# Cosine attention and feed-forward on one core: key tiles added up in float32 before the softmax totals

## The chip, the cores and the metric

The kernel runs on one core of a Trainium2 chip. The core's engines are TensorE (PE, with its weight loads as PEld), VectorE (DVE), ScalarE (ACT), GpSimd (POOL) and SyncE (SP), which issues most DMAs. The metric is the device time of one execution in microseconds. Before the change it is 416.8 us (median of three runs, 416.55 to 417.8).

## The reference

Queries, keys and values have 8 batches, 12 heads, 448 positions and 64 columns. Queries and keys are normalised, and the scores pass a softmax; the result goes through two matrices with a leaky ReLU between them.

```python
q_n = q / (np.linalg.norm(q, axis=-1, keepdims=True) + 1e-06)
k_n = k / (np.linalg.norm(k, axis=-1, keepdims=True) + 1e-06)
scores = np.matmul(q_n, k_n.transpose(0, 1, 3, 2)) / tau
scores = scores - np.max(scores, axis=-1, keepdims=True)
attn = np.exp(scores)
attn = attn / (np.sum(attn, axis=-1, keepdims=True) + 1e-09)
x = np.matmul(attn, v)                 # then (8 * 448, 768): heads side by side
h = x @ w_in                           # 768 x 2048
out = np.maximum(0.01 * h, h) @ w_out  # 2048 x 768
```

## The kernel before, in words

The order of the instructions on every engine is the order in which the Python program writes them; the framework adds the waits on semaphores. Two kinds of work are mixed by hand: attention, which needs TensorE, ScalarE, VectorE and GpSimd, and the feed-forward product, which is mostly TensorE.

The first two batches (twelve pairs of heads) go through an older path (`scores`, `totals`, `products`, `scale`). From the third batch on, the kernel works in *units* of two head pairs, 18 in all, in *groups* of one or two units, ten in all (`GROUPS`, `UNITS`). A unit has seven *key tiles*: `quad_tiles` makes the scores of 64 keys of each of its four heads by eight products of 64x32 (line 417, eight tiles of the array) into two PSUM banks, and ScalarE takes their exponential (line 423) into a bf16 tile `pe` of 128x896, kept in `pq[u, i]`.

`group_products(g, e)` (line 442) multiplies the seven tiles of a group. With `e = None` the weights are ones: the result is the sum over the keys, the softmax's denominator, from 56 products (seven tiles, four strips, two halves of the rows). With `e` 0 or 1 the weights are the even or odd columns of v. `group_logs` (line 451) and `group_inverse` (line 454) turn the sums into their inverses on ScalarE, and `group_scale` (lines 467 and 473) multiplies products and inverses on VectorE into `xT`, the feed-forward input.

The main loop runs over 42 *visits* of three key tiles. In a visit VectorE first normalises a preparation slot (`normalise`, lines 253 to 260: a slot is the queries or the keys of a unit), transposes it (line 306), and sums the squares of the next slot (line 232); SP moves the transposed tile to its place and loads a later slot. GpSimd first copies one element of the normalised tile (`hold`, line 616), which makes it wait for VectorE's multiply of line 260, and then squares the slot after next (line 216). TensorE makes one tile's scores, a *part* of a finished group if one is due, the other two tiles' scores, and then a share of feed-forward work. `parts` puts the totals (`e = None`) and the products `e = 0, 1` of a group into the visits after its last tile; `at[c]` says from which visit the chunk `c` of the feed-forward work may run, and `level` and `share` spread that work over the visits.

The feed-forward work is in eight chunks of 384 or 512 rows: `first` (line 494, six products into one bank, then the leaky ReLU on ScalarE, line 505) and `second` (line 531, sixteen products into one bank, then a copy to `osb` on VectorE, line 541, and a DMA on SP). PSUM has eight banks, dealt out by `banks`, oldest first.

After the loop come the last group's totals and products with the rest of the work, and the last chunk.

The lines that say what a sentence can't:

```python
for e in (None, 0, 1)[: 1 + len(js)]:
    last += 1
    parts[last] = (g, e)
```

Of the kernel before, what the change touches and what calls it, by code (L numbers as in the profile page):

```python
# [8 lines left out]
F32 = mybir.dt.float32  # L9
BF16 = mybir.dt.bfloat16  # L10
AF = mybir.ActivationFunctionType
ALU = mybir.AluOpType
# [4 lines left out]
def kernel(  # L17
# [10 lines left out]
    nc = tc.nc  # L28
    B, H, S, D = q.shape
# [9 lines left out]
    NQ = NPAIR // 2  # L39
# [3 lines left out]
    WARM = 20  # L43
    NEWQ = 2 * NQ
    PER = 3
    assert REM == 64 and D == 64

    ctx.enter_context(tc.manual_schedule())
    cpool = ctx.enter_context(tc.tile_pool(name="consts", bufs=1))
    ldp = ctx.enter_context(tc.tile_pool(name="ld", bufs=4))  # L50
    vbp = ctx.enter_context(tc.tile_pool(name="vb", bufs=3))
    smp = ctx.enter_context(tc.tile_pool(name="small", bufs=3))
    qnp = ctx.enter_context(tc.tile_pool(name="qn", bufs=3))
    ttp = ctx.enter_context(tc.tile_pool(name="tt", bufs=2))
    qtp = ctx.enter_context(tc.tile_pool(name="qt", bufs=6))
    pep = ctx.enter_context(tc.tile_pool(name="pe", bufs=25))
    vqp = ctx.enter_context(tc.tile_pool(name="vq", bufs=2))
    rbp = ctx.enter_context(tc.tile_pool(name="rb", bufs=2))
    xtp = ctx.enter_context(tc.tile_pool(name="xt", bufs=2))
    htp = ctx.enter_context(tc.tile_pool(name="ht", bufs=1))  # L60
    osp = ctx.enter_context(tc.tile_pool(name="os", bufs=3))
# [4 lines left out]
    gp = nc.gpsimd  # L66
# [8 lines left out]
    def banks(count, keep=None):  # L75
        lo, hi = (0, 8) if not deals["apart"] else (0, 4) if count == 2 else (4, 8)
        x = min(
            (i for i in range(lo, hi, count) if not set(range(i, i + count)) & set(kept.values())),
            key=lambda i: max(age[i : i + count]),
        )  # L80
        deals["n"] += 1
        age[x : x + count] = [deals["n"]] * count
        if keep:
            kept[keep] = x
        return ps[:, x] if count == 1 else ps[:, x : x + count]
# [31 lines left out]
    OLD = 2 * NEWQ  # L117
# [51 lines left out]
    vb, vrb = {}, []  # L169

    def load_v(j):
        if j >= B * NQ:
            return
        b, jj = divmod(j, NQ)
        vb[j] = vbp.tile([128, 4, 3, D], BF16, name="v_b")
        gp.dma_start(out=vb[j], in_=main(v, b, 4 * jj, 4))

    def load_v_rem(b, heads=range(4)):
# [9 lines left out]
    UNITS = [  # L188
        (g, (2 * js[0] + x, 2 * js[-1] + x if len(js) == 2 else 2 * js[0] + 1))
        for g, js in enumerate(GROUPS) for x in range(len(js))  # L190
    ]
# [17 lines left out]
    def squares(s, eng=gp, parts=(0, 1)):  # L209
        if s >= NSLOT:  # L210
            return
        sq = sqt[s % 3]
        if s >= OLD:
            sqs[s] = sq
            x = raw[s].rearrange("p (t d) -> p t d", d=D)
            gp.tensor_tensor(sq[:, :, :D], x, x, op=ALU.mult)  # L216
            return
        sqs[s] = halves(sq.rearrange("p t d -> p (t d)"), D + 1)
        for i in parts:
            x, y = raw[s][i], sqs[s][i]  # L220
            if eng is nc.scalar:
                nc.scalar.activation(y[..., :D], x, func=AF.Square)
            else:
                eng.tensor_tensor(y[..., :D], x, x, op=ALU.mult)  # L224
# [17 lines left out]
    def roots(s):  # L242
        if s >= NSLOT:
            return
        nc.scalar.activation(ss[s], ss[s], func=AF.Ln)  # L245
        nc.scalar.activation(norms[s % 3][:, :, 0], ss[s], func=AF.Exp, scale=0.5)  # L246
# [80 lines left out]
    pe, pr = {}, {}  # L327
# [45 lines left out]
    def totals(j):  # L373
        sm = banks(1)
        strip_products(j, sm, lambda g, ki: ones, lambda g: ones_rem[:, g // 2])
        rb = rbp.tile([128, 2, S], F32, name="rb")[:, 0]
        nc.scalar.activation(rb, sm[:, :S], func=AF.Ln)
        nc.scalar.activation(rb, rb, func=AF.Exp, scale=-1.0)
        rbs[j] = rb
# [21 lines left out]
        if (j, e) in kept:  # L401
            given_back((j, e))

    pq = {}

    def quad_tiles(which):

        tiles = []
        for u, i in which:
            sc = banks(2)  # L410
            tiles.append(sc)
            for strip in range(4):
                x = qkT[UNITS[u][1][strip // 2]]
                c0 = S + 64 * i + 32 * (strip % 2)
                for a in range(2):
                    rows = slice(64 * a, 64 * a + 64)
                    nc.tensor.matmul(  # L417
                        out=sc[32 * strip : 32 * strip + 32, a, :S], lhsT=x[rows, c0 : c0 + 32],
                        rhs=x[rows, 0:S], start=True, stop=True,
                    )  # L420
        for (u, i), sc in zip(which, tiles):
            pq[u, i] = pe_tile()
            nc.scalar.activation(out=pq[u, i], in_=sc[:, :, :S], func=AF.Exp, scale=inv_tau)  # L423

    grb = {}

    def group_products(g, e):


        us = [u for u, (gg, _) in enumerate(UNITS) if gg == g]  # L430
        two = len(us) == 2
        po = banks(2)
        for i in range(7):
            for strip in range(4):
                for w in range(2):
                    x, a = strip // 2, strip % 2
                    rows = slice(64 * w, 64 * w + 64)
                    weights = ones[rows] if e is None else (
                        vq[g][rows, strip if two else a, i]
                        .rearrange("p (d e) -> p e d", e=2)[:, e if two else w ^ x]  # L440
                    )
                    nc.tensor.matmul(  # L442
                        out=po[32 * strip : 32 * strip + 32, w, :S],
                        lhsT=weights, rhs=pq[us[x if two else 0], i][rows, a, :],
                        start=(i == 0), stop=(i == 6),
                    )
        return po

    def group_logs(g, po):
        grb[g] = rbp.tile([128, 2, S], F32, name="rb")  # L450
        nc.scalar.activation(grb[g], po[:, :, :S], func=AF.Ln)

    def group_inverse(g):
# [122 lines left out]
    sqt = []  # L576
# [11 lines left out]
    nc.vector.memset(warm, 1.0)  # L588
    ones = cpool.tile([128, 32], BF16, name="ones")
    nc.vector.memset(ones, 1.0)  # L590
    ones_rem = cpool.tile([128, 2, 32], BF16, name="ones_rem")
    nc.vector.memset(ones_rem, 0.0)
    for i in range(2):
        nc.vector.memset(ones_rem[64 * i : 64 * i + 64, i], 1.0)
    for i in range(2):
        vrb.append(cpool.tile([128, NQ, 4, D], BF16, name=f"v_rem{i}"))
        nc.vector.memset(vrb[i], 0.0)
    id128 = cpool.tile([128, 128], BF16, name="id128")
    make_identity(nc, id128)
# [264 lines left out]
    visit_of = {ui: n for n, tiles in enumerate(visits) for ui in tiles}  # L864
    parts, ready, last = {}, {}, 0
    for g, js in enumerate(GROUPS):
        last = max(last, max(visit_of[u, 6] for u, (gg, _) in enumerate(UNITS) if gg == g))
        for e in (None, 0, 1)[: 1 + len(js)]:
            last += 1
            parts[last] = (g, e)  # L870
        ready.update({j: last + 1 for j in js})
# [15 lines left out]
        for n in range(len(visits))  # L887
    ]

    held = []  # L890
    fed = 0
    for n, tiles in enumerate(visits):
        s = preps.get(n, NSLOT)
        g, e = parts.get(n, (None, None))
        scaling = e is not None

        def prepare():
            if s < NSLOT:
                transposes(s)
                load_qk(s + 4)  # L900
                hold(qn[s][:, 6, 0, 0:1])
                squares(s + 2)
                sums(s + 1)

        normalise(s)
        if not scaling:
            prepare()
        quad_tiles(tiles[:1])
        if g is not None:
            po = group_products(g, e)  # L910
            if e is None:
                group_logs(g, po)
            else:
                group_scale(g, e, po)
        if scaling:
            prepare()
        quad_tiles(tiles[1:])
        if g is not None and e is None:
            group_inverse(g)
        for u, i in tiles:  # L920
            if i == 6 and u and UNITS[u][0] != UNITS[u - 1][0]:
                load_vq(UNITS[u][0])
        for c in marked:
            if at[c] == n:
                held += marked[c]
        level = min(
            (sum(loads[c] for c in loads if at[c] <= x) - fed + sum(side[n : x + 1])) / (x - n + 1)
            for x in range(n, len(visits))
        )
        share = (level - side[n]) / (4 if n == len(visits) - 1 else 1)  # L930
        now, done = [], 0
        while held:
            w = weight(held[0][0], held[0][1][0])
            if now and done + w / 2 > share:
                break
            now.append(held.pop(0)[1][1])
            done += w
        fed += done
        for fn in now[:-1]:
            fn()  # L940
        roots(s + 1)
        for fn in now[-1:]:
            fn()
    g = len(GROUPS) - 1
    group_logs(g, group_products(g, None))
    group_inverse(g)
    rest = [fn for _, (_, fn) in held]
    cut = len(rest) // 3
    for fn in rest[:cut]:
        fn()  # L950
    for e in range(2):
        group_scale(g, e, group_products(g, e))
# [39 lines left out]
```

## Time and profile before

| | before |
|---|---|
| time, median of three runs | 416.8 us |
| the profiled execution's own time | 416.43 us |
| its span | 414.6 us |
| TensorE busy | 407.1 us, 98% of the span |
| ScalarE busy | 250.2 us, 60% |
| VectorE busy | 221.5 us, 53% |
| GpSimd busy | 114.6 us, 28% |
| the totals' products (ones, line 442) | 560 products, 15.1 us busy |
| squares of 128x896 on GpSimd (line 216) | 36, mean 1695 ns |
| multiplies of 128x896 on VectorE (line 260) | 36, mean 1176 ns |

The span is the time from the first to the last instruction that the profiler shows; the execution's time is the time of the whole run. Products on different tiles of TensorE's array can run at the same time, so the sum of busy time and the time between two starts differ. The visits run from 80.9 to 344.2 us; the last multiply of line 260 starts at 302.3 us.

### The profile page before, as it was taken

To read this page: it belongs to the slowest core of one execution; us is meant where nothing else is said; L and a number is where in the kernel's file an instruction comes from. 1 tells how busy PE (TensorE), PEld (TensorE's weight loads), DVE (VectorE), ACT (ScalarE), POOL (GpSimd) and SP (SyncE) were. 2 spreads that over 40 slices of the span, in tenths; PEclk is the share of its full clock that TensorE was granted. 3 is DMA by queue.
4 is the path that set the end of the run, shared out by engine and by line. 5 is a ranking of instruction groups with operands and counts; after the bars stand their busy time and mean duration, and the time that the engine had idled before them with its cause. 6 is when DMAs were issued, how large, how long until landed. Compare 5 with 4: busy or idle time off the path is not lost.

```text
span 414.6 us, 11342 instructions
## 1 busy us (share of the span) xinstructions
PE 407.1 (98%) x4799; PEld 212.3 (51%) x4799; DVE 221.5 (53%) x387; ACT 250.2 (60%) x431; POOL 114.6 (28%) x149
## 2 busy tenths in 40 slices
PE   8899999999999999999999999999999999999997
PEld 3335555544555555544455555554445555654565
DVE  6977976855778556766474964464621301210022
ACT  5997876378657785668865688547764464004300
POOL 4875543433234132413331433122210000000000
PEclk9999999999999999999999999999999999999999
DMA  7999998775377851884275681742442100020022
GB/s 195 242 214 220 210 234 187 181 223 129 60 206 182 204 132 22 204 229 99 53 186 157 151 229 43 175 126 84 91 90 68 51 39 3 38 77 0 2 76 76
DMA packets 41964, 53.82 MB, mean 130 GB/s; under 512 B 12474, under 2 KB 32314, under 8 KB 41914
## 3 DMA queue, kind: packets, MB, share of 16 engines
q1 hardware_dynamic: 25738, 41.01, 35.0%
q0 software_dynamic: 15488, 11.80, 19.7%
q8 instruction: 37, 0.61, 0.6%
q10 hardware_dynamic: 688, 0.30, 0.2%
q14 instruction: 13, 0.11, 0.1%
HBM read 45.61 MB, written 11.01 MB: 137 GB/s over the span
## 4 chain that ended last, share of the span: by engine, by line
PE 87%; DMA 4%; ACT 3%; DVE 3%; POOL 2%; SPq 1%; issue 1%; POOLq 0%
PE ps L531 34%; PE ps L494 34%; PE ps L442 9%; PE ps L417 7%; ACT pe L355 2%; DMA qk_h<-in_k_dram 2%; PE ps L366 2%; DVE qn L270 1%; DMA xT<-in_k_dram 1%; DMA xT<-in_q_dram 1%; POOL sq L224 1%; PE ps L346 1%; POOL sq L216 1%; DVE ss L238 0%; SPq L131 0%
## 5 line engine op out<-in xcount | busy, mean ns | idle before, releaser
L531 PE MATMUL ps<-w_out_sb,hT 128*128 128x384 bf16 (+1 forms) x912 | 151.3, 324 | 0.3 <-DVE xT L397 0.3
L494 PE MATMUL ps<-xT,w_in_sb 128*128 128x384 bf16 (+1 forms) x768 | 151.1, 353 | 0.0
L423 ACT ACTIVATE pe<-ps 128x896 bf16<-128x896 f32 x126 | 108.9, 915 | 46.1 <-PE ps L417 46.1
L531 PEld LDWEIGHTS <-hT 128*128 128x128 bf16 x912 | 86.5, 98 | 64.3 <-issue 10.0
L494 PEld LDWEIGHTS <-w_in_sb 128*128 128x128 bf16 x768 | 72.6, 98 | 74.3 <-issue 9.7
L505 ACT ACTIVATE hT<-ps 128x384 bf16<-128x384 f32 (+1 forms) x128 | 67.4, 552 | 56.0 <-PE ps L494 55.0
L541 DVE COPY osb<-ps 128x384 f32<-128x384 f32 (+1 forms) x57 | 31.2, 548 | 100.7 <-PE ps L531 100.6
L216 POOL TENSOR_TENSOR sq<-qk_h 128x896 f32<-128x896 f32 x36 | 61.0, 1695 | 9.2 <-DMA qk_h<-in_k_dram 7.7
L616 POOL CAST seen<-qn 128x1 f32<-128x1 bf16 x46 | 8.5, 185 | 169.4 <-DVE qn L260 160.5
L260 DVE TENSOR_TENSOR qn<-qk_h,r 128x896 bf16<-128x896 f32 x36 | 42.4, 1176 | 1.2
L232 DVE TENSOR_REDUCE ss<-sq 128x14 f32<-128x910 f32 x36 | 38.0, 1054 | 1.1 <-POOL sq L216 1.1
L355 ACT ACTIVATE pe<-ps 128x896 bf16<-128x896 f32 x42 | 35.9, 917 | 1.8 <-PE ps L346 1.7
L417 PE MATMUL ps<-qkT 64*32 64x448 bf16 x1008 | 36.5, 353 | 0.0
L253 DVE TENSOR_REDUCE r<-norms 128x14 f32<-128x28 f32 x48 | 8.6, 178 | 48.3 <-ACT norms L246 47.7
L467 DVE TENSOR_TENSOR xT<-ps,rb 128x448 bf16<-128x448 f32 x32 | 18.4, 617 | 23.2 <-PE ps L442 21.5
L306 DVE STREAM_TRANSPOSE tt<-qn 128x448 f32<-128x448 f32 x36 | 29.6, 821 | 0.9
L442 PE MATMUL ps<-pe,vq 64*32 64x448 bf16 x1008 | 27.0, 349 | 0.0
L245 ACT ACTIVATE ss<-ss 128x14 f32<-128x14 f32 x48 | 10.3, 214 | 25.4 <-DVE ss L232 24.4
L417 PEld LDWEIGHTS <-qkT 64*32 64x32 bf16 x1008 | 13.1, 91 | 19.2 <-issue 14.5
L442 PEld LDWEIGHTS <-vq 64*32 64x32 bf16 x1008 | 14.5, 92 | 8.0 <-issue 0.3
L442 PE MATMUL ps<-pe,ones 64*32 64x448 bf16 x560 | 15.1, 349 | 0.0
L346 PE MATMUL ps<-qkT 64*64 64x448 bf16 (+1 forms) x132 | 12.9, 359 | 2.1 <-ACT pe L355 1.2
(53 smaller groups left out, 218.9 us busy)
## 6 DMA issues: line engine op xcount, KB each, us to landing
qk_h<-in_q_dram SPq DMA_DIRECT2D x36, 224.0 KB, 4.0
qk_h<-in_k_dram SPq DMA_DIRECT2D x36, 224.0 KB, 4.3
out_dram<-osb SPq DMA_DIRECT2D x20, 384.0 KB, 2.3
qkT<-tt SPq DMA_DIRECT2D x72, 56.0 KB, 3.3
qkT<-tt SPq DMA_DIRECT2D x36, 112.0 KB, 3.5
vq<-in_v_dram POOLq DMA_DIRECT2D x16, 224.0 KB, 5.0
w_in_sb<-in_moe_w_in_dram POOLq DMA_DIRECT2D x4, 768.0 KB, 11.2
w_out_sb<-in_moe_w_out_dram POOLq DMA_DIRECT2D x2, 1536.0 KB, 22.3
```

Source lines behind the costliest of these rows:

```text
L216: gp.tensor_tensor(sq[:, :, :D], x, x, op=ALU.mult)
L232: nc.vector.tensor_reduce(ss[s], sqs[s], axis=AX.X, op=ALU.add)
L260: nc.vector.tensor_tensor(qn[s].rearrange("p m d e -> p m e d"), raw[s].rearrange(f"p ({t[1:-1]} d) -> p m e d", e=n, d=D), r.rearrange(f" ...
L306: nc.vector.transpose(out=to.rearrange(("p g (c m) -> p m g c", "p g (m c) -> p m g c")[which], m=7), in_=qn[s].bitcast(F32).rearrange("p ...
L355: nc.scalar.activation(out=dst, in_=sc[:, :, :S], func=AF.Exp, scale=inv_tau)
L417: nc.tensor.matmul(out=sc[32 * strip : 32 * strip + 32, a, :S], lhsT=x[rows, c0 : c0 + 32], rhs=x[rows, 0:S], start=True, stop=True,)
L423: nc.scalar.activation(out=pq[u, i], in_=sc[:, :, :S], func=AF.Exp, scale=inv_tau)
L442: nc.tensor.matmul(out=po[32 * strip : 32 * strip + 32, w, :S], lhsT=weights, rhs=pq[us[x if two else 0], i][rows, a, :], start=(i == 0), ...
L494: nc.tensor.matmul(out=pm[:, :n], lhsT=w_in_sb[:, kt, m * 128 : (m + 1) * 128], rhs=xT[c // 2][:, kt, c0 : c0 + n], start=(done + i == 0), ...
L505: nc.scalar.activation(out=hT[c][:, m, :n], in_=pm[:, :n], func=AF.Prelu, alpha=0.01)
L531: nc.tensor.matmul(out=po2[:, : hi - lo], lhsT=hT[c][:, m, ts * 128 : (ts + 1) * 128], rhs=w_out_sb[:, m, half * HALF + lo : half * HALF + ...
L541: nc.vector.tensor_copy(out=o[:, cols], in_=po2[:, : hi - lo])
```

## The change

In the new units, the seven exponential tiles of a unit are added up to one float32 tile of 128x896, `acc[u]`: tile one onto tile zero, and then two to six onto the sum. GpSimd makes the additions of tiles one to four in the visit of the tile, VectorE those of five and six in the visit after it. The totals of a group are then eight products (four strips, two halves of the rows) with float32 ones as weights and `acc` as the moving operand, in place of 56 bf16 products.

All parts of a group come one visit later, so chunks of the feed-forward work become free one visit later, and the seventh chunk no longer starts inside the loop; its work stands behind it. The last visit's share is no longer divided by four. In the last visit VectorE's additions follow at once.

To make room, the old path's v tiles, the v remainders and two of the three float32 sums share one tile (`shared`); the third sum lies in the third buffer of squares, so the new path's squares rotate over two buffers; one `inverse` tile takes the place of a pool of two; the pool of exponential tiles grows from 25 to 27. The float32 ones lie in the place of the identity matrix, which is no longer needed by then.

```diff
+    ADDS = {i: (nc.vector if i > 4 else nc.gpsimd) for i in range(1, 7)}
...
-    pep = ctx.enter_context(tc.tile_pool(name="pe", bufs=25))
+    pep = ctx.enter_context(tc.tile_pool(name="pe", bufs=27))
...
-        sq = sqt[s % 3]
+        sq = sqt[s % (2 if s >= OLD else 3)]
...
+    pq, acc, due, summed = {}, {}, [], set()
+
+    def add_up(eng):
+        for u, i in list(due):
+            late = u > 2 and UNITS[u - 3][0] not in summed
+            if ADDS[i] is not eng or late or (i > 1 and u not in acc):
+                continue
+            due.remove((u, i))
+            if i == 1:
+                acc[u] = totals_of[u % 3]
+            eng.tensor_tensor(
+                acc[u], pq[u, 0] if i == 1 else acc[u], pq[u, i], op=ALU.add
+            )
...
+        if e is None:
+            for strip in range(4):
+                for w in range(2):
+                    rows = slice(64 * w, 64 * w + 64)
+                    nc.tensor.matmul(
+                        out=po[32 * strip : 32 * strip + 32, w, :S], lhsT=ones_f[rows],
+                        rhs=acc[us[strip // 2 if two else 0]][rows, strip % 2, :],
+                        start=True, stop=True,
+                    )
+            summed.add(g)
+            return po
...
-        grb[g] = rbp.tile([128, 2, S], F32, name="rb")
+        grb[g] = inverse
...
+    totals_of = [
+        x.rearrange("p (a c) -> p a c", c=S) for x in (
+            shared[:, :1792].bitcast(F32), shared[:, 1792:3584].bitcast(F32),
+            sqt[2].rearrange("p t d -> p (t d)")[:, : 2 * S],
+        )
+    ]
...
-        last = max(last, max(visit_of[u, 6] for u, (gg, _) in enumerate(UNITS) if gg == g))
+        last = max(last, max(visit_of[u, 6] for u, (gg, _) in enumerate(UNITS) if gg == g) + 1)
...
+    ones_f = id128.bitcast(F32)[:, 0:32]
+    nc.vector.memset(ones_f, 1.0)
...
         quad_tiles(tiles[1:])
+        add_up(nc.vector)
+        due += [(u, i) for u, i in tiles if i]
+        add_up(gp)
...
-        share = (level - side[n]) / (4 if n == len(visits) - 1 else 1)
+        share = level - side[n]
...
+        if n == len(visits) - 1:
+            add_up(nc.vector)
...
+    rest = [fn for _, (_, fn) in held]
+    if at[B - 2] >= len(visits):
+        rest += [fn for _, (_, fn) in marked[B - 2]]
+    cut = len(rest) // 3
+    for fn in rest[:1]:
+        fn()
     group_logs(g, group_products(g, None))
     group_inverse(g)
-    rest = [fn for _, (_, fn) in held]
-    cut = len(rest) // 3
-    for fn in rest[:cut]:
+    for fn in rest[1:cut]:
         fn()
```

More of the change, by code (lines that the diff above doesn't have):

```diff
@@ L50 @@
     ldp = ctx.enter_context(tc.tile_pool(name="ld", bufs=4))
-    vbp = ctx.enter_context(tc.tile_pool(name="vb", bufs=3))
     smp = ctx.enter_context(tc.tile_pool(name="small", bufs=3))
@@ L55 @@
     qtp = ctx.enter_context(tc.tile_pool(name="qt", bufs=6))
-    pep = ctx.enter_context(tc.tile_pool(name="pe", bufs=25))
+    pep = ctx.enter_context(tc.tile_pool(name="pe", bufs=27))
     vqp = ctx.enter_context(tc.tile_pool(name="vq", bufs=2))
-    rbp = ctx.enter_context(tc.tile_pool(name="rb", bufs=2))
     xtp = ctx.enter_context(tc.tile_pool(name="xt", bufs=2))
@@ L174, in load_v @@
         b, jj = divmod(j, NQ)
-        vb[j] = vbp.tile([128, 4, 3, D], BF16, name="v_b")
+        vb[j] = v_old[:, j % 3]
         gp.dma_start(out=vb[j], in_=main(v, b, 4 * jj, 4))
@@ L375, in totals @@
         strip_products(j, sm, lambda g, ki: ones, lambda g: ones_rem[:, g // 2])
-        rb = rbp.tile([128, 2, S], F32, name="rb")[:, 0]
+        rb = inverse[:, j % 2]
         nc.scalar.activation(rb, sm[:, :S], func=AF.Ln)
@@ L402, in scale @@
             given_back((j, e))
-    pq = {}
+    pq, acc, due, summed = {}, {}, [], set()
[10 more added lines that the diff above has]
+            )
     def quad_tiles(which):
@@ L437, in group_products @@
                     rows = slice(64 * w, 64 * w + 64)
-                    weights = ones[rows] if e is None else (
+                    weights = (
                         vq[g][rows, strip if two else a, i]
@@ L590 @@
     nc.vector.memset(ones, 1.0)
+    inverse = cpool.tile([128, 2, S], F32, name="inverse")
+    shared = cpool.tile([128, 3840], BF16, name="shared")
+    v_old = shared[:, :2304].rearrange("p (j h t d) -> p j h t d", j=3, t=3, d=D)
+    totals_of = [
[4 more added lines that the diff above has]
+    ]
     ones_rem = cpool.tile([128, 2, 32], BF16, name="ones_rem")
@@ L595 @@
     for i in range(2):
-        vrb.append(cpool.tile([128, NQ, 4, D], BF16, name=f"v_rem{i}"))
+        vrb.append(shared[:, 2304 + 768 * i : 3072 + 768 * i].rearrange(
+            "p (j g d) -> p j g d", g=4, d=D
+        ))
         nc.vector.memset(vrb[i], 0.0)
```

## The prediction

> **What bounds the kernel now.** I read the busy times first, then the chain, then one attention stretch by windows, and last a few microseconds as a timeline.
>
> ```profile
> span 414.6 us, 11342 instructions
> ...
> PE 407.1 (98%) x4799; PEld 212.3 (51%) x4799; DVE 221.5 (53%) x387; ACT 250.2 (60%) x431; POOL 114.6 (28%) x149
> ...
> PE 87%; DMA 4%; ACT 3%; DVE 3%; POOL 2%; SPq 1%; issue 1%; POOLq 0%
> ...
> L216 POOL TENSOR_TENSOR sq<-qk_h 128x896 f32<-128x896 f32 x36 | 61.0, 1695 | 9.2 <-DMA qk_h<-in_k_dram 7.7
> ...
> L260 DVE TENSOR_TENSOR qn<-qk_h,r 128x896 bf16<-128x896 f32 x36 | 42.4, 1176 | 1.2
> ...
> L442 PE MATMUL ps<-pe,ones 64*32 64x448 bf16 x560 | 15.1, 349 | 0.0
> ```
>
> TensorE is busy for 98% of the span and is 87% of the chain: what leaves TensorE's queue shortens the kernel, what enters it lengthens it. The rows below it give the prices that matter: the 560 products with ones that go, and the two kinds of SBUF-to-SBUF work (a square on GpSimd, 1.695 us; a multiply on VectorE, 1.176 us) that the new additions resemble.
>
> The windows view for the stretch in which visits and preparations run together; columns are the stretch, its length, busy us of PE, PEld, DVE, ACT, POOL, the granted clock, DMA share and GB/s:
>
> ```profile
> 80.90:302.30 221.40, 221.40 (x3013) 113.87 (x3013) 139.36 (x223) 154.83 (x265) 66.50 (x79) 1.00 0.57 142
> ```
>
> TensorE has no gap here at all, at a granted clock of 1.00, while VectorE has 82 us and GpSimd 155 us to spare. One totals step in the timeline (start, length, engine, line):
>
> ```profile
> 223.69 0.38 PE L417 MATMUL ps<-qkT 64*32 64x448 bf16 x8
> ...
> 223.89 1.51 PE L442 MATMUL ps<-pe,ones 64*32 64x448 bf16 x56
> ...
> 225.21 0.56 PE L417 MATMUL ps<-qkT 64*32 64x448 bf16 x16
> 225.70 2.77 PE L531 MATMUL ps<-w_out_sb,hT 128*128 128x384 bf16 x16
> ```
>
> From 223.89 to 225.21 is 1.32 us for seven rounds of eight products, 0.189 us a round: eight tiles of the array run side by side, as one alone lasts 0.349 us. The full-array products of L531 do not overlap so: 16 take 2.6 to 2.7 us, 0.163 us each for 384 columns, 0.42 ns a column, which is also a round's 0.189 us over 448 columns. So different tiles overlap, and the same tile takes one product after the other.
>
> **The change, part by part.** The sum is made against the profiled execution, 416.43 us (span 414.6 and 1.83 around it), 0.37 below the median of 416.8.
>
> *Removed: 560 bf16 products.* Ten groups by 1.32 us, all on the path: -13.2 us.
>
> *Added: 80 float32 products, eight per group.* Built, each becomes two weight loads and two products on one and the same tile, one right behind the other (160 pairs in TensorE's program). No row of before has a float32 product. Lower bound: the 16 run as two side-by-side rounds at the bf16 rate, 0.38 us a group. Upper bound: all 16 one after the other and twice the time per column (four bytes for two), 16 x 0.377 = 6.0 us. I take the value by the row nearest to it, same-tile products that do not overlap (L531): the second of a pair waits for the first, products start in order, so the next tile's first starts beside it; eight steps of 0.377 us and a last one half covered by the following scores, 3.2 us. Ten groups: +32.0 us; ends +3.8 and +60.3.
>
> The Trainium skill's page "FP8 and Floating Point Precision", section TensorE Precision Notes, says that true float32 takes four passes through the array. By it, with eight tiles side by side, a group would take four rounds, an estimate of 0.75 us, and the sum would come out 5.7 us below before; no run here shows it yet.
>
> *Added: 72 additions of 128x896 on GpSimd (four of a unit's six) and 36 on VectorE.* GpSimd: the square's row, 1.68 us, also two operand reads and one write; 72 x 1.68 = 121 us. VectorE: the multiply's 1.18 us; 36 x 1.18 = 42 us. None is on TensorE; the cover is the spare time above. In the stretch 80.90 to 302.30 fall 64 and 32 of them: GpSimd 66.5 + 107.5 = 174 us, VectorE 139.4 + 37.8 = 177 us, against 221.4 - 8 x 1.32 + 8 x 3.2 = 236 us of TensorE. Each fits by itself. Together they may not, because the two engines hold each other up here:
>
> ```profile
> 62.02 1.17 DVE L260 TENSOR_TENSOR qn<-qk_h,r 128x896 bf16<-128x896 f32 x1
> ...
> 62.53 2.16 POOL L216 TENSOR_TENSOR sq<-qk_h 128x896 f32<-128x896 f32 x1 [3.64 <-DMA qk_h<-in_k_dram]
> ...
> 66.26 1.68 POOL L216 TENSOR_TENSOR sq<-qk_h 128x896 f32<-128x896 f32 x1 [1.44 <-DMA qk_h<-in_q_dram]
> ```
>
> The square that met a multiply for 0.66 us lasted 0.48 us longer than the next one; 0.18 us of it stayed hidden. Now the `hold` copies keep such meetings rare; the additions have no hold. Taken one at a time, GpSimd's 174 and VectorE's two-input 37.7 + 37.8 make 249.5 us; less 0.18 us for each of 95 GpSimd operations, 17 us, 232 us. That is just inside 236, so I take no overhang, and 1.3 us for uneven visits (short ones of 4.7 us against 7.3 us). Bounds: 0, and 249.5 - 236 = +14.
>
> *New waits.* The totals on TensorE wait for the unit's last addition on VectorE; behind them stand 16 score products and the visit's feed-forward work, and ScalarE's log and exponentials wait for them. VectorE's addition five waits for GpSimd's four; behind it stand the copies that free PSUM, the next normalisation, and through the hold the next squares. The totals come two visits after a unit's last tile, the VectorE additions one, so they have a visit of 4.7 to 7.3 us less the 3.4 us chain of normalise, transpose and sums: covered, and priced in the 1.3 us; without that cover a late addition costs up to 1.7 us a group, 17 us.
>
> *Parts a visit later.* Log (0.92 us) and inverse (0.96) on ScalarE, products on TensorE, scalings (0.58 each) on VectorE keep their number and only meet other visits; they issue no DMA, and loads and stores on SP's and GpSimd's queues keep their visits, though the v loads on GpSimd's now stand near additions. The e-tiles live a visit (three tiles) longer with two buffers more: one tile of slack less, 0; one exponential, 0.92 us, a group if that is gone. Squares rotate over two buffers: the one reused is read by a sum that stands on VectorE before the multiply which GpSimd's hold waits for, so 0. The shared tile for old v and sums, one inverse buffer, one 85 ns fill: 0, hidden under TensorE.
>
> *End.* The seventh chunk's work moves wholly behind the visits, the same products. Between the last scores and the last totals stand 16 second products and six first, 2.7 + 1.0 us, against two exponentials and two additions, 1.8 + 2.4 us: +0.5 us; bounds 0 and +3.
>
> Sum: 416.4 - 13.2 + 32.0 + 1.3 + 0.5 = 437.0 us.
>
> **Rivals.**
>
> *A. Side by side (other side, faster).* If the eight tiles' pairs overlap fully, a group's totals take between 0.38 and 0.75 us (two rounds, at twice the time per column for the latter), the path loses 5.7 to 9.4 us and, with the additions covered, the time is 407 to 411 us. For: eight bf16 tiles do overlap. Against: the pairs stand together in the queue, and same-tile products follow each other. It decides where a group's float32 products take under 1.3 us.
>
> *B. Cheap products, blocked additions.* With A's products the stretch would need only 221.4 - 8 x 0.57 = 217 us of TensorE, and the 232 us of GpSimd and VectorE taking turns become the bound: 416.4 - 5.7 + 15 = 426 us (421 to 432). For: the 62.53 square. Against: 0.18 us may hide more.
>
> The Trainium skill states this in "SBUF — State Buffer", section SBUF: two separate sides: GpSimd and a VectorE instruction with two SBUF inputs share one port pair under an exclusive lock. The trace agrees, with the 2.16 us square beside 1.68.
>
> *C. Both dear.* All 16 products in a row (6.0 us, +28 over mine), or my products and the full 14 us of turns: 451 to 465 us. For: the lone product's 0.349 us. Against: adjacent products of different tiles start together in every bf16 round.
>
> *D. A draw*, products at about 1.3 us and covered additions: 416 to 417 us.
>
> **How the numbers follow.** Forecast 0.50 (its own range 430 to 446), A 0.17, B 0.17, C 0.12, D 0.04. Faster by over 0.3% (about what this kernel's runs can tell from no change) is A, 0.17; within it D, 0.04; slower the rest, 0.79. The range leaves out the upper part of C and the lower edge of A: 409 to 450, which holds some 0.83.
>
> **What would show it.** A float32 row with 160 products at the totals' line and about 3.2 us from the first of a group to the next scores; under 1.3 us is A. GpSimd's additions at 1.7 us, some at 2 to 3; TensorE waiting at the totals for VectorE's sum by 1 to 2 us in all; over 10 is B or C. Multiplies of 1.18 us stretched where additions run. In the end stretch, second and first products in unchanged number. I would be wrong most easily in the products' overlap, which no row of before shows for this type.

## The result, and the profile after

The changed kernel takes 450.76 us (median of four runs, 449.42 to 452.07) against 417.04 us for the kernel before on the same chips: the ratio is 1.081, 95% interval 1.077 to 1.084. The change makes it slower by about 34 us. The profiled execution has a span of 450.26 us, 35.6 us more than the 414.64 of before. The direction was forecast; the time lies just over the top of the range (450), and the mechanism is not the one that the forecast was built on.

From the page of the changed kernel: span, busy times, the chain by engine, and the groups that answer to those shown of before.

```profile
span 450.3 us, 10724 instructions
...
PE 413.4 (92%) x4383; PEld 211.2 (47%) x4399; DVE 299.6 (67%) x424; ACT 250.3 (56%) x431; POOL 278.2 (62%) x221
...
PE 62%; DVE 18%; DMA 11%; issue 3%; ACT 2%; POOL 2%; SPq 1%; DVEq 0%; POOLq 0%
...
L413 POOL TENSOR_TENSOR shared<-shared,pe 128x896 f32<-128x896 f32 x36 | 79.6, 2212 | 4.3 <-ACT pe L434 2.4
L215 POOL TENSOR_TENSOR sq<-qk_h 128x896 f32<-128x896 f32 x36 | 62.4, 1733 | 4.5 <-DMA qk_h<-in_k_dram 3.2
L259 DVE TENSOR_TENSOR qn<-qk_h,r 128x896 bf16<-128x896 f32 x36 | 57.5, 1597 | 1.2
```

TensorE is no longer busy all the time (92% for 98%), and VectorE's share of the chain (the work that ended last, followed back) rose from 3% to 18%. The multiply that took 1.176 us now takes 1.597 us on the mean, although nothing about it was changed.

The totals in the timeline of the changed kernel (start, length, engine, line):

```profile
250.98 0.38 PE L428 MATMUL ps<-qkT 64*32 64x448 bf16 x8
...
251.18 0.55 PE L448 MATMUL ps<-sq,id 64*32 64x448 f32 x4
...
251.19 0.55 PE L448 MATMUL ps<-shared,id 64*32 64x448 f32 x4
...
251.55 0.55 PE L448 MATMUL ps<-sq,id 64*32 64x448 f32 x4
...
251.57 0.55 PE L448 MATMUL ps<-shared,id 64*32 64x448 f32 x4
...
251.93 0.56 PE L428 MATMUL ps<-qkT 64*32 64x448 bf16 x16
```

From 251.18 to the next scores at 251.93 is 0.75 us for all 16 float32 products, where 56 bf16 products took 1.32 us. The eight first products start together, and the eight second ones together 0.376 us later. So each lasts two bf16 rounds of 0.189 us, side by side on eight tiles. Five of the ten groups take 0.75 us; the other five take 0.94 to 6.3 us, because the sum of one of their units came late. Without that wait TensorE itself gained 0.57 us a group.

So the loss lies elsewhere. By the traces' windows, it lies in the stretch from the first scores of the visits to the end of the last multiply: 80.89 to 303.75 us before, 82.03 to 335.23 after. (The last multiply of before starts at 302.6 us, not at 302.3 as the section on the profile before has it.) The time ahead of the stretch grew by 1.1 us, the stretch by 30.3 (222.9 to 253.2), what follows by 4.1 (110.9 to 115.0): 35.6 together. The windows of the changed kernel, columns as before:

```profile
82.03:335.23 253.20, 226.34 (x2686) 112.34 (x2697) 210.26 (x254) 154.39 (x265) 208.78 (x141) 0.95 0.51 124
```

TensorE is idle for 27 of these 253 us, and the granted clock is 0.95 for 1.00. VectorE and GpSimd are busy for 83% and 82% by their durations, which now hold time spent waiting for the other. Laid over each other, GpSimd's instructions and VectorE's with two inputs from SBUF (multiplies and additions) cover 239 of the 253 us; before it was 105 of 223. One of the worst places in the timeline:

```profile
260.68 7.41 DVE L413 TENSOR_TENSOR shared<-shared,pe 128x896 f32<-128x896 f32 x2
...
260.93 1.70 POOL L215 TENSOR_TENSOR sq<-qk_h 128x896 f32<-128x896 f32 x1
...
262.57 1.88 POOL L413 TENSOR_TENSOR sq<-pe 128x896 f32<-128x896 bf16 x1
264.52 5.30 POOL L413 TENSOR_TENSOR sq<-sq,pe 128x896 f32<-128x896 f32 x2
268.01 0.54 DVE L563 COPY osb<-ps 128x384 f32<-128x384 f32 x1
...
268.61 0.58 PE L428 MATMUL ps<-qkT 64*32 64x448 bf16 x8 [6.86 <-DVE osb L563]
...
269.12 4.03 PE L553 MATMUL ps<-w_out_sb,hT 128*128 128x384 bf16 x16
```

Two VectorE additions that need 1.09 us each take 7.41 us, while GpSimd works through a square and three additions without a pause. The copy behind them (268.01), which frees a PSUM bank, is late, and TensorE waits 6.86 us for it. The 16 products at 269.12 then take 4.03 us for 2.77: the clock was halved from 264.9 us for 6.8 us by the profiler's clock record. In all it was halved for 23.9 us in five spells, each beside a wait of TensorE of 2.65 to 6.86 us: four of these waits were for a copy on VectorE, one for a sum. The Trainium skill's page "TensorE: Matmul & The Clock Gate", Part 1, says that TensorE falls to half its clock after an idle window of about 3.4 us. The trace agrees with the window: the spells last 3.41 or 6.83 us, and their starts lie whole multiples of 3.41 us apart. It does not agree that a whole window of idleness is needed: waits of 2.65 and 3.09 us were enough.

Mean durations by whether an instruction overlapped in time with one of the other engine that reads two inputs from SBUF ("met") or not ("alone"), from the two traces, in us; the number of instructions stands in brackets:

| | alone | met | longest |
|---|---|---|---|
| GpSimd addition, after (72) | 1.887 (19) | 2.375 (53) | 2.82 |
| VectorE addition, after (36) | 1.09 (4) | 1.97 (32) | 4.73 |
| VectorE multiply, after (36) | 1.171 (12) | 1.810 (24) | 2.80 |
| VectorE multiply, before (36) | 1.177 (35) | 1.166 (1) | 1.21 |

### The profile page after: what moved, and what is told of

The parts are those of the page before. It is cut to its first block, busy times and chain, and to the rows that moved or that the text cites. A ratio compares the mean times of both kernels' runs of the same rounds, so it can differ in the third digit from the quotient of the medians.

```text
span 450.3 us, 10724 instructions
## 1 busy us (share of the span) xinstructions
PE 413.4 (92%) x4383; PEld 211.2 (47%) x4399; DVE 299.6 (67%) x424; ACT 250.3 (56%) x431; POOL 278.2 (62%) x221
## 3 DMA queue, kind: packets, MB, share of 16 engines
q1 hardware_dynamic: 25738, 41.01, 33.7%
## 4 chain that ended last, share of the span: by engine, by line
PE 62%; DVE 18%; DMA 11%; issue 3%; ACT 2%; POOL 2%; SPq 1%; DVEq 0%; POOLq 0%
PE ps L516 28%; PE ps L553 23%; DMA w_out_sb<-in_moe_w_out_dram 5%; PE ps L428 4%; DVE shared L413 4%; PE ps L464 3%; DVE qn L259 3%; DVE sq L413 2%; DVE ss L231 2%; DVE tt L305 2%; DMA qk_h<-in_k_dram 2%; PE ps L448 2%; DVE osb L563 1%; DVE xT L489 1%; DMA qkT<-tt 1%
## 5 line engine op out<-in xcount | busy, mean ns | idle before, releaser
L553 PE MATMUL ps<-w_out_sb,hT 128*128 128x384 bf16 (+1 forms) x912 | 157.4, 332 | 4.3 <-DVE osb L563 3.5
L553 PEld LDWEIGHTS <-hT 128*128 128x128 bf16 x912 | 88.6, 100 | 72.5 <-issue 19.8
L413 POOL TENSOR_TENSOR shared<-shared,pe 128x896 f32<-128x896 f32 x36 | 79.6, 2212 | 4.3 <-ACT pe L434 2.4
L259 DVE TENSOR_TENSOR qn<-qk_h,r 128x896 bf16<-128x896 f32 x36 | 57.5, 1597 | 1.2
L428 PE MATMUL ps<-qkT 64*32 64x448 bf16 x1008 | 41.4, 358 | 13.0 <-DVE osb L563 10.5
L413 DVE TENSOR_TENSOR shared<-shared,pe 128x896 f32<-128x896 f32 x24 | 44.5, 1854 | 7.3 <-POOL shared L413 7.0
L413 POOL TENSOR_TENSOR sq<-sq,pe 128x896 f32<-128x896 f32 x18 | 42.8, 2380 | 1.0
L649 POOL CAST seen<-qn 128x1 f32<-128x1 bf16 x46 | 10.4, 225 | 51.6 <-DVE qn L259 38.8
L413 POOL TENSOR_TENSOR shared<-pe 128x896 f32<-128x896 bf16 x12 | 25.3, 2112 | 11.8 <-ACT pe L434 11.7
L489 DVE TENSOR_TENSOR xT<-ps,inverse 128x448 bf16<-128x448 f32 x32 | 18.2, 614 | 17.8 <-PE ps L464 17.8
```

Of the source, the lines that this page charges most:

```text
L259: nc.vector.tensor_tensor(qn[s].rearrange("p m d e -> p m e d"), raw[s].rearrange(f"p ({t[1:-1]} d) -> p m e d", e=n, d=D), r.rearrange(f" ...
L413: eng.tensor_tensor(acc[u], pq[u, 0] if i == 1 else acc[u], pq[u, i], op=ALU.add)
L428: nc.tensor.matmul(out=sc[32 * strip : 32 * strip + 32, a, :S], lhsT=x[rows, c0 : c0 + 32], rhs=x[rows, 0:S], start=True, stop=True,)
L553: nc.tensor.matmul(out=po2[:, : hi - lo], lhsT=hT[c][:, m, ts * 128 : (ts + 1) * 128], rhs=w_out_sb[:, m, half * HALF + lo : half * HALF + ...
```

## The experiments

The leading theory was: GpSimd's additions and VectorE's two-input instructions take turns at SBUF, VectorE falls behind, and TensorE starves (the *turns* theory). Its rivals: the new order costs by itself (*order*); VectorE or GpSimd have too much to do without holding each other up (*backlog*). Six of the kernels below were timed once: those with one engine's additions small, with the fills, with the copies on ScalarE (both) and with all additions on VectorE. For a sense of the noise, the four runs of the changed kernel span 449.4 to 452.1 us, and the eight of the new order alone 417.9 to 420.1.

**Small additions on one or both engines.** In three kernels the additions of both engines, of GpSimd or of VectorE work on 8 of 448 columns, so that the sums are left out; everything else stays but for one added fill. The angle brackets stand for the condition of each kernel.

```diff
-            eng.tensor_tensor(
-                acc[u], pq[u, 0] if i == 1 else acc[u], pq[u, i], op=ALU.add
-            )
+            n = 8 if <this engine's are small> else S
+            eng.tensor_tensor(
+                acc[u][:, :, :n], (pq[u, 0] if i == 1 else acc[u])[:, :, :n], pq[u, i][:, :, :n], op=ALU.add
+            )
```

> All additions work on 8 of 448 columns (16 elements a row), so the sums are left out but every instruction, wait and place in the order stays; one fill of the shared tile is added. Turns theory (GpSimd's additions and VectorE's instructions with two SBUF inputs hold each other up, VectorE falls behind and TensorE starves): the loss is gone, and what is left is the float32 products' gain of 5.7 us: 410 to 412 us. Order theory (the later parts and the moved feed-forward work cost by themselves): 420 us or more. The backlog theory (the engines have too much to do, without holding each other up) also says 410 to 412.

> Only GpSimd's 72 additions are small; VectorE's 36 stay whole. Turns theory: VectorE is held up only by the 36 squares as before: 410 to 413 us. A theory by which VectorE's own 36 additions and their place ahead of the PSUM copies are the cost: 425 us or more.

> Only VectorE's 36 additions are small; GpSimd's 72 stay whole. Turns theory: GpSimd's additions still meet VectorE's 33 multiplies, so a part of the loss stays: 418 to 438 us, with multiplies longer than 1.2 us. If VectorE's additions alone are the cost: 410 to 413.

Measured: both small, 414.63 us (ratio to before 0.994, 0.992 to 0.996); VectorE's whole, 421.73; GpSimd's whole, 427.43; all whole, 450.76. With both small the kernel is faster than before, but by 2.2 us, not by 5 to 7. VectorE's 36 additions alone cost 7.1 us, which the turns theory had put at 0 to 1: 421.73 lies between its 413 and its rival's 425, so both expectations missed, and backlog has a part. GpSimd's 72 alone cost 12.8, inside the expected 418 to 438 us, and the multiplies are stretched as expected (median 1.63 us, longest 2.81). Both together cost 36.1, 16 us more than the two apart: the two engines' work does not add up, it interferes.

**GpSimd equally busy, but not reading.** Each GpSimd addition becomes two fills of the same tile, so GpSimd's part of the sums is left out.

```diff
+            if eng is gp:
+                for _ in range(2):
+                    gp.memset(acc[u], 1.0)
+                continue
```

> Each of GpSimd's 72 additions is replaced by two fills of the sum's tile, which should take about 1.7 us together, as long as an addition, but read nothing from SBUF; VectorE's additions and their wait for GpSimd stay. GpSimd's part of the sums is left out. Turns theory, if the two engines share a way to read SBUF: no hold-up, 410 to 414 us at the same GpSimd load. Backlog theory (GpSimd is late by its own load): still 430 us or more. If writing is held up too: 430 or more with VectorE's multiplies stretched.

Measured: 424.28 us, 10 over the turns theory's upper end and 6 under backlog's lower end, and 26.5 below the changed kernel. TensorE and GpSimd's fills on its page, and VectorE's multiplies from the view of one line (its name, count, and shortest, median and longest duration in ns):

```profile
span 422.5 us, 10719 instructions
...
PE 406.1 (96%) x4399; PEld 208.6 (49%) x4399; DVE 256.6 (61%) x424; ACT 249.3 (59%) x431; POOL 233.5 (55%) x293
...
L415 POOL MEMSET shared<- 128x896 f32 x96 | 80.7, 844 | 4.2
...
L415 POOL MEMSET sq<- 128x896 f32 x48 | 40.5, 844 | 9.2 <-PE ps L452 7.0
```

```profile
L259 DVE TENSOR_TENSOR qn<-qk_h,r x36: 1160/1170/1208, 62.3 to 305.0; 128x896 bf16<-128x896 f32 x36
```

GpSimd has 121 us of extra work (its additions would have 136 without stretching), VectorE's additions wait for it as in the changed kernel, and yet no multiply is longer than 1.21 us and no addition longer than 1.25. What stretches VectorE is GpSimd reading SBUF, not GpSimd being busy. The two kernels differ in one thing more: a fill does not wait for an exponential. That hardly frees VectorE: its additions wait for GpSimd's part 6.5 us in all here, and 7.5 us in the changed kernel.

TensorE has the same products in both kernels, so the two pages also tell what the 27.8 us between their spans are. TensorE's idle time, the span less its busy time, is 16.4 us with fills and 36.9 us in the changed kernel: some 20 us are waiting. The other 7 are products that take longer (413.4 us busy for 406.1; 16 of the changed kernel's products have no record). The halved clock explains them: it lasts 3.4 us with fills and 23.9 in the changed kernel, and 5.7 of those pass while TensorE waits, so the difference costs (18.2 - 3.4) / 2 = 7.4 us.

**The PSUM copies on ScalarE.** Are late copies the way in which VectorE's lateness reaches TensorE? The same edit was made in the changed kernel and in the one where only VectorE's additions are whole.

```diff
-            nc.vector.tensor_copy(out=o[:, cols], in_=po2[:, : hi - lo])
+            nc.scalar.copy(out=o[:, cols], in_=po2[:, : hi - lo])
```

> The changed kernel, with the 57 copies that free the feed-forward product's PSUM banks on ScalarE (whole run) in place of VectorE; all additions stay. If TensorE's idle time comes from these copies standing behind additions that are held up: the 17.6 us of waits on them and most of the 11.9 us of halved clock go, 422 to 432 us. If the totals themselves or the preparations are late: 440 us or more.

> The run with GpSimd's additions small and VectorE's whole (421.7 us), with the PSUM copies on ScalarE. If those 7.1 us over the small additions on both engines are copies standing behind VectorE's additions: 414 to 416 us. If they are late totals or preparations: 420 or more.

Measured: 447.24 us and 420.06 us; only 3.5 and 1.7 us came back, which for single runs is little more than the noise. The copies are one way among several: in the first of the two TensorE now waits 9.1 us for VectorE's scalings of a group and about 7 us for the copies on ScalarE. The waits of the changed kernel with copies on ScalarE (who waited for whom, total us, times, longest), and one case in its timeline:

```profile
ACT ss L244 <- DVE ss L231: 52.7, 19, 9.4
...
POOL seen L649 <- DVE qn L259: 39.1, 22, 5.8
```

```profile
117.42 5.89 DVE L413 TENSOR_TENSOR shared<-shared,pe 128x896 f32<-128x896 f32 x2
...
127.76 0.21 ACT L244 ACTIVATE ss<-ss 128x14 f32<-128x14 f32 x1 [6.95 <-DVE ss L231]
...
128.12 0.46 ACT L563 COPY osb<-ps 128x384 f32<-128x384 f32 x1
...
128.63 4.44 PE L553 MATMUL ps<-w_out_sb,hT 128*128 128x384 bf16 x16 [4.68 <-ACT osb L563]
```

ScalarE's logarithm of the sums of squares waits up to 9.4 us for VectorE, and behind it in ScalarE's queue stand the next exponentials and now the copies. At 127.76 us it has waited 6.95 us, the copy behind it is late, and TensorE has lost 4.68 us when the copy is done. The lateness of one engine's queue passes to the next, whichever of them does the copy.

**The order by itself.** The changed kernel without additions, with the bf16 products of before.

```diff
-                    weights = (
+                    weights = ones[rows] if e is None else (
...
-        add_up(nc.vector)
-        due += [(u, i) for u, i in tiles if i]
-        add_up(gp)
```

> The changed kernel's order (parts a visit later, moved feed-forward work, shared tiles) with no additions and with the 56 bf16 products with ones a group of before. If the order costs by itself what the small additions left over: 418 to 421 us. If the order is free: 416 to 417, and the small-additions run's missing 3.5 us belong to its waits.

Measured: 419.08 us, ratio 1.0041 (1.0026 to 1.0055), which is 1.7 us. The new order costs a little. From it to the small additions is a gain of 4.5 us. The cheaper products alone should give 5.7 us; that the small additions and their waits take the rest was not tested.

**All additions on VectorE.** This takes GpSimd out and keeps the number of additions.

```diff
-    ADDS = {i: (nc.vector if i > 4 else nc.gpsimd) for i in range(1, 7)}
+    ADDS = {i: nc.vector for i in range(1, 7)}
```

> All 108 additions on VectorE (1.09 us each), a visit late; GpSimd has its squares alone, as in the kernel before. VectorE then has 139 us of before and some 101 us of additions in the stretch in which TensorE has 217: if it can't fill every gap, VectorE is the bound: 432 to 447 us, with TensorE waiting for VectorE. Turns theory: additions last 1.1 us on the average and GpSimd's squares 1.7, few stretched. If the engine's load did not matter, only turns: 411 to 418.

Measured: 458.75 us, 12 above the expectation's upper end. Windows from 82 to 330 us:

```profile
82.00:330.00 248.00, 220.03 (x2596) 109.30 (x2580) 228.83 (x308) 151.39 (x258) 66.31 (x79) 0.97 0.52 126
```

Here VectorE is busy 229 of 248 us with nearly unstretched instructions (additions 1.09 to 1.24 us on the mean, multiplies 1.20). So backlog is real too: enough load alone costs as much as the turns. The additions have to be cheaper, not only somewhere else.

**A version that beats both.** From the kernel before: VectorE adds tiles in pairs, in bf16, and the totals are four bf16 rounds (three pair sums and the seventh tile) in the visits of before.

```diff
+            pairs[u, i // 2] = pair_of[3 * (u % 2) + i // 2]
+            nc.vector.tensor_tensor(pairs[u, i // 2], pq[u, i - 1], pq[u, i], op=ALU.add)
...
-        for i in range(7):
+        for i in range(7) if e is not None else (1, 3, 5, 6):
...
         for fn in now[:-1]:
             fn()
+        add_pairs(tiles)
```

> A version from the kernel before: VectorE adds key tiles 0 and 1, 2 and 3, 4 and 5 of each unit in bf16 (54 additions), at the end of a visit between its PSUM copies; GpSimd adds nothing, and the totals are four rounds of bf16 products in place of seven, in the same visits as before. Turns theory: three rounds of 0.189 us less in ten groups, 5.7 us, and little lost since only squares meet the additions: 410 to 413 us. If VectorE's queue is as tender as with its whole float32 additions: 415 to 420.

Measured: 414.51 us, between the two expectations; the ratio to before is 0.9931 (0.9916 to 0.9946), 2.8 us less than the 417.31 of before beside it. The rounds saved are worth 5.7 us; half of it stays. The groups show why the price is low:

```profile
L412 DVE TENSOR_TENSOR shared<-pe 128x896 bf16<-128x896 bf16 x36 | 23.6, 670 | 1.7 <-ACT pe L431 1.5
...
L412 DVE TENSOR_TENSOR sq<-pe 128x896 bf16<-128x896 bf16 x18 | 12.5, 703 | 2.3 <-ACT pe L431 2.3
```

A bf16 addition takes 0.615 us alone against 1.09 for the float32 sum, and 54 of them fill 36 us of VectorE. One addition more a unit, for three rounds:

```diff
+            if i == 3:
+                nc.vector.tensor_tensor(pairs[u, 0], pairs[u, 0], pairs[u, 1], op=ALU.add)
...
-        for i in range(7) if e is not None else (1, 3, 5, 6):
+        for i in range(7) if e is not None else (1, 5, 6):
```

> The pair sums with one more bf16 addition a unit (pair 0 and 1 to a four), so three rounds of products in place of four: TensorE 1.9 us less, VectorE 11 us more. 412 to 414 us if VectorE still has room; over 415 if its queue is the limit.

Measured: 416.43 us, ratio 0.9979 (0.9966 to 0.9991): 1.9 us less for TensorE, and yet some 2 us slower than four rounds, as expected if VectorE's queue is the limit. Eleven microseconds more of VectorE (18 additions of 0.62) cost more than they bring.

## Why the prediction was right and wrong

*Removed products, -13.2 us:* right. The 560 products are gone, at 1.32 us a group.

*Float32 products, +32.0 us:* wrong, and the step that carried the forecast. It failed where the prediction said that "products start in order, so the next tile's first starts beside it". Both products of a pair stand together in the queue, but the eight tiles' first products start within 0.02 us and the second ones 0.376 us later: tiles run beside each other across pairs. Where no wait comes between, ten groups are 7.5 us in place of 32.0. The Trainium skill's page "FP8 and Floating Point Precision", section TensorE Precision Notes, states four passes through the array for true float32. The trace agrees: two products of two bf16 rounds each, 0.75 us, which is the estimate that the prediction made from the page and did not use. The prediction had both rows, tiles that overlap and a tile that does not, and let the second decide.

*Additions, "no overhang":* wrong, and the error in the products hid it. The turns were right in kind and near in size: 232 us estimated, 239 measured as covered time, the addition being 1.887 us in place of 1.68. They were held against 236 us of TensorE, 25 of which were the float32 products that never came. Against the 215 us which the stretch takes with small additions, the overhang is 24 us by the prediction's own method. On top come 14 us of the stretch in which neither engine of the pair has such an instruction.

*Waits "covered, and priced in the 1.3 us":* wrong. At the totals alone TensorE lost some 9 us, the time by which five groups exceed 0.75 us, and 17.6 us more at the PSUM copies. VectorE's whole additions without GpSimd's cost 7.1 us, with GpSimd's load 9.7, with its reading 36.1. The prediction named the copies, the normalisation and the totals behind a late addition, but took the mean load of VectorE as if its queue could use any gap. It did not name ScalarE's logarithms of the squares' sums, which carry the lateness on.

*Parts a visit later, 0:* nearly; 1.7 us by the run of the order alone. *End, +0.5 us:* right in size; the last totals take 1.01 us for 0.75 in the trace of the changed kernel.

*Rivals.* The mechanism is rival B, cheap products and blocked additions, given 0.17 and 426 us. Its price was low: 15 us of overhang for 24, and nothing for the idle time that turns leave on queues that depend on each other, or for the halved clock. Rival A's product price was right, 0.75 us a group; the run with small additions is what it describes, at 414.6 us in place of 407 to 411: of the 5.7 us 3.5 are missing, 1.7 of them by the new order. The forecast of 437 came nearer to 450.8 than B's 426 only because one error stood in for another; that is luck.

The steps from before to after, each from its run: order +1.7, float32 products with small additions -4.5, VectorE's additions +7.1, GpSimd's load +2.6, GpSimd's reading beside VectorE +26.5. They come to 33.4, and the measured difference is 33.7. The steps are differences between runs beside slightly different medians of before (416.8 to 417.5), and two of the runs are single, so each is good to 1 or 2 us, and the 2.6 us of GpSimd's load is hardly clear of that. Of the last step about a quarter is the halved clock, by the two pages shown with the fills; it follows from the waits.

## What to carry to other kernels

Before work is moved to GpSimd "because it is idle", add the time of its instructions that read SBUF to that of VectorE's instructions with two SBUF inputs and hold the sum against the bounding engine's time: here each engine fitted alone, and the pair did not. Check that sum also against the time that the change is meant to reach, not against a time that another guess has made longer. Where a reduction on TensorE is to be shortened, make the additions cheap first (bf16 pairs at 0.615 us) and leave the rest of the rounds on TensorE.

## What was not expected of the hardware

Float32 products of 64x32 tiles overlap fully: 16 products of eight tiles in 0.75 us, each tile's second 0.376 us after its first, although the pairs are adjacent in the program.

VectorE did not get every second turn. An addition of VectorE whose record starts at 260.68 us waited for a square and then for the addition behind it, which had started (262.57) before the square had ended (260.93 + 1.70 = 262.63); it lasted 4.73 us. GpSimd's own additions are stretched by 0.49 us on the mean when they meet one, VectorE's by 0.88.

The Trainium skill's page "SBUF — State Buffer", section SBUF: two separate sides, says that whoever starts first has the shared ports for the whole instruction, and that a VectorE instruction with two SBUF inputs is held only by a GpSimd instruction that reads SBUF. The traces agree with the second: 144 fills left the multiplies at 1.16 to 1.21 us. They agree with the first in nearly all cases: in the changed kernel 32 squares, additions and multiplies of 128x896 started while the other engine had none of this kind and were joined by one later, and 31 of them kept their time within 0.06 us. The exception is the addition at 260.68 us, whose record starts 0.25 us before that of the square for which it waited; why is open.
